# Preparing the second batch's second half later in the third chunk, with VectorE's and GpSimd's order held as written, in an attention kernel followed by an MLP

## The chip, the cores and the metric

The kernel runs on one core of one Trainium2 chip. The metric is the time of one execution on the device, in microseconds; lower is better. Times are given as the median of several executions. The profile and the trace come from one further execution of the same program.

## The reference

There are four batches, eight heads, 768 positions and 64 values per head. Queries and keys are hashed by the signs of six projections, and a query attends only to keys with the same six signs. The result goes through a layer norm, two matrix products with a rectifier between (512 to 2048 to 512), and a residual sum.

```python
q_bits = (np.einsum('bhsd,dk->bhsk', q, proj) > 0)        # the same for k
mask = q_bucket[:, :, :, None] == k_bucket[:, :, None, :]
scores = np.where(mask, scale * q @ k.T, -1e9)
attn = softmax(scores); x = attn @ v                       # heads side by side: 512 wide
xn = (x - mean) / sqrt(var + 1e-6) * g_ln
out = x + np.maximum(xn @ w_ch1, 0) @ w_ch2
```

## The kernel before

The work is cut into 12 chunks, numbered from 0: three for each batch, each with 256 query rows of all eight heads. A chunk's attention is 12 units, three for each pair of heads. A unit is `scores` (TensorE, L435), `exps` (ScalarE, L445), `values` (TensorE, L469, called av) and, after each third unit, `divide` (VectorE, L487 to L497). Scores and exponentials of the next unit are written ahead of the values of this one.

Between the units of chunk n the kernel places other work, called fillers:

- `norm` of chunk n-1: VectorE takes statistics (L516, L517) and writes xn (L518), for each of two rows; a transposing DMA on SyncE's queue, SP, makes xnT (L538); GpSimd makes rs, the inverse deviation (L529, L530). For chunk 1 the transposes are done by TensorE (`xtrans`, L550) and copied by VectorE (L557).
- eight `down` steps of chunk n-2 (L590, four products each). The last of each four is followed by L595, in which VectorE takes the sum o out of PSUM, and by a store.
- eight `up` steps of chunk n-1 (L566, eight products each), whose results VectorE (L576) and ScalarE (L578) rectify in turn.
- preparation of a later batch, by half (four heads). A step's letter is followed by batch and half, so that N11 is the narrowing of batch 1, half 1, which is the second batch's second half.

The preparation's letters: L and W load queries, keys, and values (SP's queue); Q takes squares on ScalarE; N narrows queries and keys to bf16 on GpSimd (two casts, L282); B transposes 32-wide blocks on VectorE (four, L287); T issues a transposing DMA on SP and a copy from it (L304, L309); H is 32 hash products on TensorE (L318), two VectorE instructions for the bits (L326, L329), and one store and four loads on SP (L331, L333); V casts values (L344) and sums them (L351, L353) on GpSimd; E is one product on TensorE (L358, share) and a VectorE copy (L359). Products of hashes, shares, xnT's transposes, ups and downs all take one of two PSUM buffers with the tag mm.

`plan` says what chunk n prepares. What stands before the bar is spread over the first four downs, what stands behind it over the last four, and `interleave` then places the whole list by the costs given with each step (a down counts 870, an up 900, hash products 1300, a share 110, the rest nothing). The rest of the written order is in `interleave`: a unit's scores and exponentials, fillers, values, divide, fillers.

The written order is binding only where `tc.manual_schedule` holds an engine. In chunks 0 and 1 (`first_two`) all engines are held. From chunk 2 on only ScalarE is held, and the framework's scheduler chooses at build time the order in which the other engines and SP's queue get their instructions. `tc.no_sync_barrier()` stands between the chunks. The norm, downs and ups after the last chunk stand outside any held block.

Chunk 9 ends with `safety`: VectorE reduces the squares (L647), TensorE transposes the result (L650), and VectorE makes a flag of it (L652 to L656). It costs 0 in the list and stands last in it.

```python
fillers = [norm]
fillers += mixed(early, tail[:4]) + ([(600, xtrans)] if n == 2 else [])
fillers += mixed(late, tail[4:]) + ups
...
with tc.manual_schedule(engines={mybir.EngineType.Activation}):
    interleave(units[n], fillers, after, single)
```

Of the kernel before, what the change touches and what calls it, by code (L numbers as in the profile page):

```python
# [30 lines left out]
def kernel(  # L31
# [629 lines left out]
    def interleave(units, fillers, after=None, single=()):  # L661

        total = sum(c for c, _ in fillers) or 1
        slots_n = 2 * len(units)
        done, fi = 0.0, 0

        def fill(upto):
            nonlocal done, fi  # L670
            while fi < len(fillers) and done <= upto * total:
                c, f = fillers[fi]
                f()
                done += c
                fi += 1

        for u, (_, _, values, divide) in enumerate(units):
            nxt = units[u + 1] if u + 1 < len(units) else after
            if nxt:
                nxt[0]()  # L680
                nxt[1]()
            fill((2 * u + 1) / slots_n)
            if u % 2 and u // 2 < len(single):
                for _, f in single[u // 2]:
                    f()
            values()
            divide()
            fill((2 * u + 2) / slots_n)
        while fi < len(fillers):
            fillers[fi][1]()  # L690
            fi += 1
# [4 lines left out]
    def chunk_tile():  # L696
        return work.tile([P, TT, d_model], F32, tag="x", bufs=3, name="x")
# [18 lines left out]
    def first_two():  # L716
# [76 lines left out]


    plan = {
        2: "H10 N11 B11 V10 W11 | T11 H11 E10 V11 W20",
        3: "E11 N20 B20 | T20 H20",
        4: "V20 W21 B21 N21 | T21 H21 E20",
        5: "V21 W30 | E21",
        6: "V30 W31 N30 B30 | T30 H30 E30",  # L800
# [7 lines left out]
    def prepare(text):  # L808
        return [
            step  # L810
            for op in text.split()
            for step in preps[int(op[1])].part(op[0], half=int(op[2]))
        ]

    def mixed(a, b):

        tagged = [((i + 1) / (len(a) + 1), 0, i, s) for i, s in enumerate(a)]
        tagged += [((i + 1) / (len(b) + 1), 1, i, s) for i, s in enumerate(b)]
        return [s for *_, s in sorted(tagged, key=lambda e: e[:3])]
# [6 lines left out]
    for n in range(2, len(chunks)):  # L826
        tc.no_sync_barrier()
        mlp[n - 1] = mlp_steps(*chunks[n - 1], xs[n - 1])
        norm, ups, downs, xtrans, _ = mlp[n - 1]
        early, late = (prepare(part) for part in (plan.get(n, "") + "|").split("|")[:2])  # L830
# [3 lines that stand above are left out]
        tail = downs  # L834
        if n == NT * (B - 1):
            fillers.append((0, safety))
        after = None
        if n + 1 < len(chunks):
            xs[n + 1] = chunk_tile()
            units[n + 1] = att_units(*chunks[n + 1], xs[n + 1])  # L840
            after = units[n + 1][0]
        single = [[step] for step in prepare(singly.get(n, ""))]
        if len(single) > 4:
            single[3:] = [sum(single[3:], [])]
        with tc.manual_schedule(engines={mybir.EngineType.Activation}):
            interleave(units[n], fillers, after, single)
    tc.no_sync_barrier()
    norm, ups, downs, _, _ = mlp_steps(*chunks[-1], xs[len(chunks) - 1])
# [188 lines left out]
```

## Time and profile before

| what | value |
|---|---|
| three runs | 321.61, 322.49, 322.43 us, median 322.43 |
| the profiled execution | 322.48 us |
| its span in the profile | 320.6 us |
| TensorE busy | 303.1 us, 95% of the span |
| ScalarE, VectorE, GpSimd busy | 216.6, 186.8, 85.0 us |
| DMA | 40.93 MB, 128 GB/s on average |

The span runs from the first to the last instruction of the profile; what lies around it makes up the rest of the execution's time. In the profile PE is TensorE's products and PEld its weight loads, DVE is VectorE, ACT ScalarE, POOL GpSimd, and SPq SyncE's queue, which issues most of the DMAs. L435 is line 435 of the kernel. An arrow in brackets behind a timeline row gives the idle time of that engine just before it, and what ended it. The granted clock is TensorE's, as a share of full speed. A busy TensorE is not TensorE at its peak, since its products are pipelined and their ends are modelled.

### The profile page before, as it was taken

The page shows a single profiled execution, that of the slowest core. Times are in us where ns is not written, and L with a number is a line of the kernel's source. Part 1 is how long each engine was busy: PE and PEld are TensorE (multiplying, and loading weights), DVE is VectorE, ACT ScalarE, POOL GpSimd, SP SyncE. Part 2 cuts the span into 40 slices and gives each one's busy share as a digit, 9 for nine tenths or more (in the row PEclk, how much of TensorE's full clock was granted, in tenths as well). Part 3 has the DMA queues.
Part 4 walks back from the last instruction along what each step waited for, and adds up shares of the span by engine and source line. Part 5 has one row for each costly group of instructions (what it writes and reads, how often), then busy time and mean ns, then how long its engine had stood idle before and what let it go on. Part 6 is the DMA issues. An engine that isn't in the chain of part 4 may idle for free.

```text
span 320.6 us, 7775 instructions
## 1 busy us (share of the span) xinstructions
PE 303.1 (95%) x3225; PEld 226.5 (71%) x3252; DVE 186.8 (58%) x403; ACT 216.6 (68%) x272; POOL 85.0 (27%) x110
## 2 busy tenths in 40 slices
PE   7979999799999998999999999999999999999991
PEld 6566687469669656868768768769679688686650
DVE  1799987833893772456596675543634734446320
ACT  4677976558668764778778678779788568564110
POOL 3467522850330280057082040100200200201000
PEclk9999999989999997999999999999999999999997
DMA  7999999978577597824984452020120210200301
GB/s 249 353 199 301 209 341 109 152 193 177 166 145 212 154 171 195 251 75 147 255 129 81 84 111 60 2 69 34 30 72 2 65 35 2 65 35 2 99 13 63
DMA packets 64826, 40.93 MB, mean 128 GB/s; under 512 B 47136, under 2 KB 59680, under 8 KB 64784
## 3 DMA queue, kind: packets, MB, share of 16 engines
q1 hardware_dynamic: 60368, 31.85, 41.5%
q0 software_dynamic: 4128, 8.13, 10.9%
q8 instruction: 27, 0.44, 0.6%
q10 hardware_dynamic: 288, 0.39, 0.3%
q14 instruction: 15, 0.12, 0.1%
HBM read 27.98 MB, written 6.88 MB: 109 GB/s over the span
## 4 chain that ended last, share of the span: by engine, by line
PE 81%; DVE 12%; DMA 2%; ACT 1%; issue 1%; POOL 0%; SPq 0%; POOLq 0%
PE hp L566 27%; PE o L590 20%; PE sc L435 17%; PE av L469 10%; DVE xn L518 3%; PE hash L318 3%; DMA xnT<-xn 2%; DVE bt L287 2%; PE tpose L200 2%; DVE slots L262 2%; PE wakep L731 1%; DVE slots L238 1%; DVE stats L516 1%; PE hash L252 1%; DVE x L497 1%
## 5 line engine op out<-in xcount | busy, mean ns | idle before, releaser
L445 ACT ACTIVATE ex<-sc,expb 128x1024 bf16<-128x1024 f32 x144 | 159.4, 1113 | 65.1 <-PE sc L435 62.6
L566 PE MATMUL hp<-xnT,w_sb 128*128 128x256 bf16 x768 | 99.8, 274 | 2.6 <-DMA xnT<-xn 2.3
L590 PE MATMUL o<-w_sb,hbuf 128*128 128x512 bf16 x357 | 92.6, 379 | 3.3 <-DVE x L595 2.2
L435 PE MATMUL sc<-slots 70*128 70x256 bf16 x576 | 87.0, 273 | 2.4 <-POOL slots L238 1.5
L566 PEld LDWEIGHTS <-w_sb 128*128 128x128 bf16 x768 | 72.2, 98 | 12.1 <-DMA xnT<-xn 3.0
L469 PEld LDWEIGHTS <-ex 128*128 128x128 bf16 x1152 | 54.5, 98 | 16.0 <-issue 1.5
L576 DVE TENSOR_SCALAR hbuf<-hp 128x512 bf16<-128x512 f32 x48 | 33.1, 690 | 54.6 <-PE hp L566 54.4
L435 PEld LDWEIGHTS <-slots 70*128 70x128 bf16 x576 | 52.1, 97 | 17.1 <-issue 3.7
L469 PE MATMUL av<-vaug,ex 128*128 128x65 bf16 x1152 | 59.2, 194 | 0.3 <-ACT ex L445 0.2
L590 PEld LDWEIGHTS <-hbuf 128*128 128x128 bf16 x384 | 35.5, 97 | 30.1 <-issue 2.6
L529 POOL TENSOR_SCALAR rs<-mv 128x2 f32<-128x2 f32 x12 | 6.3, 523 | 144.2 <-DVE mv L517 144.0
L578 ACT ACTIVATE hbuf<-hp 128x512 bf16<-128x512 f32 x48 | 28.5, 594 | 18.7 <-PE hp L566 18.5
L595 DVE SCALAR_TENSOR_TENSOR x<-o,rs,x 128x512 f32<-128x512 f32 x24 | 17.8, 741 | 34.5 <-PE o L590 34.5
L518 DVE SCALAR_TENSOR_TENSOR xn<-x,mv,gbc 128x512 bf16<-128x512 f32 x24 | 21.7, 927 | 0.1
L497 DVE TENSOR_TENSOR x<-x,rc 128x256 f32<-128x256 f32 x36 | 19.0, 529 | 0.9
L282 POOL CAST nat<-qnat 128x1536 bf16<-128x1536 f32 x6 | 9.0, 1501 | 36.4 <-DMA qnat<-in_q_dram 24.6
L516 DVE BATCH_NORM_STATS2 stats<-x 128x6 f32<-128x512 f32 x24 | 15.4, 681 | 0.3
L490 DVE TENSOR_TENSOR x<-av,vsum 128x256 f32<-128x256 f32 x36 | 14.9, 414 | 0.0
L489 DVE TENSOR_SCALAR rc<-av 128x4 f32<-128x4 f32 x36 | 5.7, 158 | 15.7 <-PE av L469 15.7
L344 POOL CAST vaug<-vnat 128x1536 bf16<-128x1536 f32 x8 | 11.8, 1474 | 8.0 <-PE av L469 4.0
L180 ACT ACTIVATE knat<-knat 128x768 f32<-128x768 f32 x16 | 13.4, 835 | 0.0
L180 ACT ACTIVATE qnat<-qnat 128x768 f32<-128x768 f32 x16 | 13.3, 833 | 0.0
(83 smaller groups left out, 215.1 us busy)
## 6 DMA issues: line engine op xcount, KB each, us to landing
out_dram<-x SPq DMA_DIRECT2D x24, 256.0 KB
vnat<-in_v_dram SPq DMA_DIRECT2D x7, 768.0 KB
qnat<-in_q_dram SPq DMA_DIRECT2D x11, 384.0 KB
knat<-in_k_dram SPq DMA_DIRECT2D x11, 384.0 KB
w_sb<-in_moe_w_ch_dram POOLq DMA_DIRECT2D x4, 1024.0 KB, 14.0
slots<-slots SPq DMA_DIRECT2D x6, 384.0 KB
qnat<-in_q_dram POOLq DMA_DIRECT2D x2, 768.0 KB, 14.5
knat<-in_k_dram POOLq DMA_DIRECT2D x2, 768.0 KB, 15.9
```

The lines of the kernel that those rows point to most:

```text
L180: nc.scalar.activation(src, src, AF.Square, accum_out=sq[:, a, col : col + 1],)
L435: nc.tensor.matmul(sc[:, i, :], key_block(h, kj), query_blocks(h),)
L445: nc.scalar.activation(ex, sc, AF.Exp, bias=expb[:, 1:2] if b else expb[:, 0:1], scale=scale if b else scale / Q_SCALE,)
L469: nc.tensor.matmul(av[:, h - ha, qi, :], state[g][:, i, qi * P : (qi + 1) * P], va[:, h, kj, :], start=(b > 0 and (g, i, qi) == (0, 0, 0)) ...
L497: nc.vector.tensor_tensor(xv, num, rc.unsqueeze(3).to_broadcast([P, 2, TT, D]), op=AOP.mult)
L516: nc.vector.bn_stats(stats, x[:, i, :])
L518: nc.vector.scalar_tensor_tensor(xn[:, :, i, :], x[:, i, :].rearrange("p (o d) -> p o d", d=P), mv[:, i, 0:1], gbc.rearrange("p (o d) -> p ...
L566: nc.tensor.matmul(hp[:, i, :], w1_sb[:, dt, nt * P : (nt + 1) * P], st["xnT"][:, dt, :], start=(dt == 0), stop=(dt == ND - 1),)
L576: nc.vector.tensor_scalar_max(dst, src, 0.0)
L578: nc.scalar.activation(dst, src, AF.Relu)
L590: nc.tensor.matmul(o2, st["h"][:, nt, i * P : (i + 1) * P], w2_sb[:, nt, :], start=(nt == 0), stop=(nt == NH - 1),)
L595: nc.vector.scalar_tensor_tensor(x[:, i, :], o2, st["rs"][:, i : i + 1], x[:, i, :], op0=AOP.mult, op1=AOP.add,)
```

## The change

Two edits. In chunk 2 the steps V10, W11, B11 and N11 move behind the bar, in this order, so that they are spread over the last four downs, ahead of T11, H11, E10 and V11; of the early ones only H10 stays before the bar. W20 moves from the end of chunk 2 to the start of chunk 3. And from chunk 2 on the written order is binding for VectorE and GpSimd as well as for ScalarE; TensorE and SP are left to the scheduler as before.

```diff
     plan = {
-        2: "H10 N11 B11 V10 W11 | T11 H11 E10 V11 W20",
-        3: "E11 N20 B20 | T20 H20",
+        2: "H10 | V10 W11 B11 N11 T11 H11 E10 V11",
+        3: "W20 E11 N20 B20 | T20 H20",
         4: "V20 W21 B21 N21 | T21 H21 E20",
...
-        with tc.manual_schedule(engines={mybir.EngineType.Activation}):
+        with tc.manual_schedule(
+            engines={
+                mybir.EngineType.Activation, mybir.EngineType.DVE, mybir.EngineType.Pool
+            }
+        ):
             interleave(units[n], fillers, after, single)
```

## The prediction

> **What bounds the kernel now.** I read the page's busy table first, then the windows cut at the chunk boundaries, then the list of waits, then the timeline of the two stretches that stand out. Chunks are counted from 0 as in the code; chunk 2 is the third.
>
> ```profile
> PE 303.1 (95%) x3225; PEld 226.5 (71%) x3252; DVE 186.8 (58%) x403; ACT 216.6 (68%) x272; POOL 85.0 (27%) x110
> ```
>
> TensorE is the bound, with 17.5 us idle in 320.6. An order can only win where TensorE stands still or is throttled, so I cut the span where each chunk's first BATCH_NORM_STATS2 starts (columns: us, then busy us of PE, PEld, DVE, ACT, POOL, granted clock, DMA share, GB/s).
>
> ```profile
> 51.80:82.60 30.80, 28.44 (x321) 20.88 (x323) 17.38 (x31) 19.12 (x26) 13.95 (x16) 0.94 0.78 160
> 82.60:107.40 24.80, 24.30 (x272) 18.29 (x275) 17.43 (x36) 18.69 (x26) 8.07 (x7) 1.00 0.60 149
> 107.40:135.20 27.80, 25.63 (x272) 18.87 (x274) 15.93 (x36) 18.61 (x25) 7.15 (x9) 0.94 0.84 208
> 205.10:227.30 22.20, 22.09 (x240) 17.00 (x240) 10.70 (x29) 18.21 (x25) 1.71 (x2) 1.00 0.13 38
> ```
>
> The last row is chunk 8, with nothing to prepare: 22.2 us is the floor. Chunk 4 has one set of hash products (1.5 us) and a share (0.3) more, so about 24.0; it took 27.8. Chunk 2 has two sets, two shares, 0.6 of transposes and 0.6 of extra av products, so about 27.0; it took 30.8. Chunk 3 is 0.8 over. From chunk 5 on nothing is lost. So some 8 us can be won, nearly all in chunks 2 and 4. The timeline names the causes:
>
> ```profile
> 58.15 1.03 PE L590 MATMUL o<-w_sb,hbuf 128*128 128x512 bf16 x4
> 59.56 1.82 DVE L287 STREAM_TRANSPOSE bt<-knat 128x768 f32<-128x768 f32 x2
> 61.83 0.74 DVE L595 SCALAR_TENSOR_TENSOR x<-o,rs,x 128x512 f32<-128x512 f32 x1
> 62.62 1.02 PE L590 MATMUL o<-w_sb,hbuf 128*128 128x512 bf16 x3 [2.20 <-DVE x L595]
> ```
>
> Chunk 2: the first o was complete at 59.2, but L595, which empties its PSUM buffer, stood behind block transposes (L287) that the scheduler had put ahead of it; TensorE waited 2.20 us.
>
> ```profile
> 111.34 0.71 DVE L518 SCALAR_TENSOR_TENSOR xn<-x,mv,gbc 128x512 bf16<-128x512 f32 x1
> 113.44 3.69 SPq L304 DMA_TRANSPOSE slots<-nat  x1
> 117.23 1.26 SPq L538 DMA_TRANSPOSE xnT<-xn  x1
> 121.62 1.64 PE L566 MATMUL hp<-xnT,w_sb 128*128 128x256 bf16 x8 [2.01 <-DMA xnT<-xn]
> ```
>
> Chunk 4: xn was ready at 112.05, but its transposing DMA stood on SP behind that of L304, which itself waited for GpSimd's cast until 113.40. TensorE waited 2.01 us. Each hole also costs clock:
>
> ```profile
> 60.48:63.90 3.42, 1.22 (x7) 1.00 1.10 213
> 118.51:121.92 3.41, 1.40 (x11) 1.00 1.14 157
> 19.52:22.94 3.42, 1.91 (x18) 1.00 1.09 183
> ```
>
> (us, PE busy, clock.) After the first two stretches the clock is half for 3.41 us, 63.9 to 67.3 and 121.9 to 125.3: half of 3.41, 1.7 us, each. After the third, busy 1.91 of 3.42, it stays full.
>
> The Trainium skill ("TensorE: Matmul & The Clock Gate", Part 1) has the clock halve after an idle window of about 3.4 us. By that rule gaps of 2 us would cost no clock and 3.4 us less could be won (about 321.8 in place of the forecast below); the granted 0.94 in both chunks contradicts it, so the rows decide and it gets no chance.
>
> **The change, part by part.** The sum is made against the profiled execution's own 322.48 us (span 320.6, 1.9 outside), 0.05 above the median.
>
> *Chunk 2, plan and VectorE's order.* Written out, VectorE's order is: both norm rows, bits of H10, divide of unit 2, L595 of the first o, copy of xnT, then the four blocks. L595 then starts when the o ends and TensorE has scores, eight transposes and one unit's av (1.25 us) to run meanwhile. The casts N11, beside which the two xn took 3.76 us (1.40 where GpSimd was quiet), move behind values and sums. Gain: 2.2 + 1.7 = 3.9. What is late next: H11 needs the four blocks, which now start near 60.6 and end near 64.4 (4 x 0.95), against a written place near 63.8 on TensorE. Bounds: 0, if the hash is queued behind other ready products, to 2.2, the old hole; I take 0.5, nearest to the 0.2 to 0.3 that hashes waited before.
>
> *Moved steps at nothing.* H10 passes two groups of down products; its bits still reach SP by about 57.5 instead of 61.7 and are needed only at the end of chunk 2. T11 (SP 3.7 to 4.2 us, then the copy L309) moves from 57.4 to about 64 on SP; bits of H11, its store and four loads stay near 68 to 77; the half is needed by unit 6 of chunk 3, near 89: 10 us of cover, beyond which each us would stop TensorE. W11 leaves SP some 4 us earlier, since values10 is done sooner. W20, a SP load, moves from 72.5 to chunk 3's start; its values are cast only in chunk 4. V11's sums finish near 69, share 11 comes near 81.
>
> *Chunk 3.* The four loads L20 stand on SP behind the bits of H11 in both versions (77.07 to 79.15), so they land at about the same absolute time, K by 86.4 at the latest; but chunk 3 starts some 3 us sooner. Held VectorE then waits at the blocks, with L595 and a divide behind it: last block near 89.7, against about 88.8 where TensorE reaches H20. Loss 0 to 2; I take 0.9, less 0.3 of the present excess: +0.6.
>
> *Chunk 4.* GpSimd's written order is rs of the norm, values20, its sums, then the two casts of N21. So the cast can no longer be scheduled ahead of the norm, and the scheduler, which still orders SP, sees xnT ready 8 us before L304. The norm without blocks between takes about 3.2 us (2 x (0.65 + 0.16 + 0.75)), xnT leaves near 3.3 us into the chunk instead of 9.6, and lands 4.35 later, before the ups at 12. Gain 2.0 + 1.7 = 3.7.
>
> *Chunks 4, 6, 7, the held queues.* GpSimd used to run values and sums ahead, in chunks 3 and 5; now all of it (9 us: 1.3 + 1.5 + 3.4 + 3.0) follows the norm. The four blocks come before or around L595, so the hash can be late by what VectorE loses. Bounds 0 to 2.2 each; I take 0.3 each, 0.9 in all.
>
> *Chunk 9, safety.* It is written last, behind unit 11's divide, and VectorE is now held.
>
> ```profile
> 242.16 0.19 DVE L647 TENSOR_REDUCE m<-sq 128x2 f32<-128x32 f32 x1 [0.46 <-ACT knat L180]
> 248.17 0.38 PE L650 MATMUL mp<-identf,m 128*1 128x128 f32 x2
> 248.37 0.16 DVE L489 TENSOR_SCALAR rc<-av 128x4 f32<-128x4 f32 x1 [1.12 <-PE av L469]
> ```
>
> The reduction L647 was done 6 us early. Now it starts after the divide that begins at 248.37 and takes 1.0, ends near 249.6, and mp can start at 249.65 instead of 248.17. Engines do not cross chunk barriers (VectorE idled 2.1 us before 154.6, with a block of chunk 6 ready), so TensorE waits: +1.5. Its stretch stays about 58% busy, where the clock held. If scores of chunk 10 could pass, it would be 0; if the clock drops, 3.2.
>
> *Chunks 8, 10, 11* show VectorE already in written order, apart from interleaved norm rows: 0. The last norm stands outside the held block.
>
> Sum: -3.9 + 0.5 + 0.6 - 3.7 + 0.9 + 1.5 = -4.1, so 318.4.
>
> **Rivals.** (a) Only chunk 4's hole closes; chunk 2's moves to H11 at its full size: -3.7 + 0.6 + 0.9 + 1.5 = -0.7, 321.8. For it: the blocks are four in a row just before the hash; against it: downs and scores are ready to fill. (b) The held queues cost nothing and safety hides: -7.6, 314.9; against it: 242.16 and 248.17 above. (c) Slower: GpSimd's bunched run beside VectorE. x L497 took 1.58 us at 164.83 beside a cast, 0.42 alone, and xn 1.88 against 0.70. If in chunks 3, 4, 6 and 7 this makes L595 and blocks late at a TensorE order that doesn't allow for it, each loses 2.2 and, where a stretch falls under half busy, 1.7: four times 2.2 and once 1.7 is 10.5 in place of the 1.5 counted, +4.9, 327.4. It decides from 5.6 lost there, 1.4 a chunk. The Trainium skill ("SBUF — State Buffer", on the shared port pair) says a VectorE instruction with two SBUF inputs and a GpSimd one that reads SBUF exclude each other for a whole instruction; the trace agrees (1.58 against 0.42). Against (c): block transposes keep 0.94 to 0.97 either way. (d) The order changes nothing: excluded, since the trace's order differs from the written one at both holes.
>
> **Numbers.** Forecast 0.56, own range 316.5 to 320.5; (a) 0.16, two thirds of it faster by over 0.3%; (b) 0.05; (c) 0.21, part of it only just slower; the rest, 0.02, is cancellation. Faster 0.70, same 0.08, slower 0.22. 0.3% (1 us) is about what a measurement of this kernel tells from no change. The range runs from 315.5 to 323.6, leaving out most of (b) and (c).
>
> **What would show it.** Right: no wait of PE o L590 on DVE x L595 and none of PE hp on xnT before the last chunk, granted clock 1.00 in chunks 2 and 4, about 27.7 and 24.3 us for them, L538 before L304 in chunk 4, m after the last divide of chunk 9 with 1.5 us of idle TensorE before mp. Wrong: a clock of 0.5 anywhere between 50 and 290 us, hash products that wait over 1 us, or TensorE waiting for slots.

## The result, and the profile after

The changed kernel takes 323.38 us (median of 20 executions, 321.41 to 325.53), the kernel before 322.14 (20 executions, 320.57 to 323.87). The ratio is 1.0045 with a 95% interval of 1.0023 to 1.0066: it is slower by about half a per cent, where the prediction had it 1.3% faster. (The comparisons leave disturbed executions out, so a ratio need not be the quotient of two medians.) The profiled execution of after took 325.0 us, 323.0 of them span; it is one of the longer ones.

The page's busy table first:

```profile
PE 303.6 (94%) x3252; PEld 225.3 (70%) x3252; DVE 188.2 (58%) x403; ACT 216.6 (67%) x272; POOL 84.3 (26%) x110
```

TensorE is busy as long as before and idle 19.4 us in place of 17.5: the sum says nothing of what happened. The windows do. These are chunks 2 to 7 and 9 of after, cut where VectorE's last divide of the chunk before ends; chunk 9 is cut at the end of L654, a step of `safety`, where that comes later (columns: us, busy us of PE, PEld, DVE, ACT, POOL, granted clock, DMA share, GB/s):

```profile
52.14:79.33 27.19, 27.19 (x325) 20.20 (x324) 16.35 (x31) 19.47 (x27) 13.65 (x16) 1.00 0.60 142
79.33:105.78 26.45, 24.78 (x276) 18.40 (x275) 15.83 (x35) 18.61 (x25) 4.38 (x4) 1.00 0.80 187
105.78:130.42 24.64, 24.04 (x275) 18.04 (x273) 17.63 (x35) 18.32 (x25) 9.07 (x10) 1.00 0.81 185
130.42:156.59 26.17, 24.08 (x243) 17.74 (x241) 11.50 (x30) 18.16 (x25) 6.22 (x8) 0.93 0.52 154
156.59:181.41 24.82, 24.48 (x275) 18.12 (x273) 16.96 (x36) 18.34 (x25) 9.24 (x10) 1.00 0.50 117
181.41:206.05 24.64, 24.02 (x275) 18.02 (x273) 17.66 (x35) 18.31 (x25) 9.08 (x10) 1.00 0.41 88
228.23:251.63 23.40, 22.09 (x242) 17.07 (x240) 11.73 (x31) 17.75 (x25) 1.49 (x2) 1.00 0.13 35
```

In the first row TensorE is busy all of the time at full clock. The dip to 0.94 in chunks 2 and 4 is gone, and a dip to 0.93 stands in chunk 5. Cut in the same way, the chunks of all the kernels take (us, from one profiled execution each; chunk 8 takes 22.15 to 22.18 and chunk 11 takes 21.71 to 21.73 in every one). The prediction's cuts lie up to 0.25 us earlier, so its rows for chunks 2 to 4 of before differ a little from the first row here.

| kernel | c2 | c3 | c4 | c5 | c6 | c7 | c9 | c10 |
|---|---|---|---|---|---|---|---|---|
| before | 31.03 | 24.73 | 27.64 | 22.26 | 23.82 | 23.82 | 22.41 | 22.26 |
| after | 27.19 | 26.45 | 24.64 | 26.17 | 24.82 | 24.64 | 23.40 | 22.60 |
| e1_plan_only | 28.54 | 25.08 | 27.58 | 22.28 | 23.81 | 23.81 | 22.40 | 22.27 |
| e2_hold_only | 27.36 | 27.85 | 24.65 | 26.37 | 24.80 | 24.65 | 23.41 | 22.60 |
| e3_pool_free | 27.20 | 24.34 | 24.41 | 22.27 | 26.40 | 24.15 | 23.42 | 22.60 |
| e4_share_later | 27.19 | 25.99 | 24.64 | 22.16 | 25.17 | 24.63 | 23.41 | 22.60 |
| e5_safety | 27.19 | 25.30 | 24.64 | 24.52 | 24.82 | 24.64 | 22.57 | 22.15 |
| e6_chunk3_late | 27.19 | 24.21 | 26.01 | 26.17 | 24.79 | 24.63 | 23.41 | 22.60 |
| e7_three | 27.19 | 24.66 | 27.97 | 22.16 | 25.18 | 24.65 | 22.56 | 22.15 |
| e8_all_late | 27.19 | 24.21 | 25.45 | 22.16 | 25.40 | 25.39 | 22.57 | 22.16 |
| e9_dve_to_four | 27.19 | 24.53 | 24.15 | 22.28 | 23.80 | 23.82 | 22.40 | 22.27 |
| e10_both_to_four | 27.19 | 26.11 | 24.66 | 22.28 | 23.81 | 23.81 | 22.40 | 22.27 |
| e11_pool_not_five | 27.19 | 26.04 | 24.64 | 22.28 | 24.81 | 24.64 | 23.42 | 22.59 |
| e12_dve_old_plan | 28.55 | 24.62 | 24.16 | 22.27 | 23.82 | 23.80 | 22.40 | 22.26 |

The second row less the first: chunk 2 -3.84, chunk 4 -3.00, together -6.84 won; chunk 3 +1.72, chunk 5 +3.91, chunks 6 and 7 +1.82, chunks 9 and 10 +1.33, together 8.78 lost; with 0.34 before chunk 2 that is +2.3 of the 2.4 us between the spans.

The two holes of before are closed. Chunk 2, the timeline:

```profile
59.62 0.75 DVE L595 SCALAR_TENSOR_TENSOR x<-o,rs,x 128x512 f32<-128x512 f32 x1 [0.29 <-PE o L590]
60.60 1.03 PE L590 MATMUL o<-w_sb,hbuf 128*128 128x512 bf16 x4
61.05 1.83 DVE L287 STREAM_TRANSPOSE bt<-qnat 128x768 f32<-128x768 f32 x2
64.41 1.51 PE L318 MATMUL hash<-bt,proj 128*32 128x192 f32 x32
```

L595 now waits for the o, not the o for L595; the blocks come behind it, and the hash products behind those without a wait. Chunk 4, VectorE and SP's queue:

```profile
108.37 0.75 DVE L518 SCALAR_TENSOR_TENSOR xn<-x,mv,gbc 128x512 bf16<-128x512 f32 x1
109.19 1.30 SPq L538 DMA_TRANSPOSE xnT<-xn  x1
118.00 3.65 SPq L304 DMA_TRANSPOSE slots<-nat  x1
```

The transpose of xn leaves SP 0.07 us after xn is ready and 8.8 us ahead of L304, behind which it stood before.

What took their place is in the list of TensorE's waits (us in total, times, longest):

```profile
PE share L358 <- POOL vs L353: 2.1, 1, 2.1
...
PE hash L318 <- DVE x L595: 1.4, 3, 1.0
PE mp L650 <- DVE m L647: 1.3, 1, 1.3
PE hp L566 <- DVE vsum L359: 1.1, 3, 0.4
...
PE hash L318 <- DVE bt L287: 0.7, 1, 0.7
```

The largest, 2.1 us at a share, is in chunk 5, where the prediction had looked for nothing.

### The profile page after: what moved, and what is told of

Its sections match the earlier page's. It is cut to its first block, busy times and chain, and to the rows that moved or that the text cites. A ratio compares the mean times of both kernels' runs of the same rounds, so it can differ in the third digit from the quotient of the medians.

```text
span 323.0 us, 7803 instructions
## 1 busy us (share of the span) xinstructions
PE 303.6 (94%) x3252; PEld 225.3 (70%) x3252; DVE 188.2 (58%) x403; ACT 216.6 (67%) x272; POOL 84.3 (26%) x110
## 4 chain that ended last, share of the span: by engine, by line
PE 65%; DVE 15%; DMA 9%; POOL 5%; ACT 2%; issue 2%; SPq 0%; POOLq 0%; DVEq 0%; ACTq 0%
PE hp L566 24%; PE o L590 15%; PE sc L435 13%; PE av L469 8%; DVE bt L287 2%; DVE xn L518 2%; DVE stats L516 2%; PE hash L318 2%; DMA proj<-in_proj_dram 2%; DMA qnat<-in_q_dram 2%; DVE x L497 2%; DMA slots<-nat 2%; DVE slots L262 2%; DMA slots<-slots 1%; POOL vsum L353 1%
## 5 line engine op out<-in xcount | busy, mean ns | idle before, releaser
L566 PE MATMUL hp<-xnT,w_sb 128*128 128x256 bf16 x768 | 98.7, 272 | 1.6 <-DVE vsum L359 1.1
L590 PE MATMUL o<-w_sb,hbuf 128*128 128x512 bf16 x384 | 97.4, 382 | 0.0
L529 POOL TENSOR_SCALAR rs<-mv 128x2 f32<-128x2 f32 x12 | 9.1, 759 | 193.1 <-DVE mv L517 193.1
L595 DVE SCALAR_TENSOR_TENSOR x<-o,rs,x 128x512 f32<-128x512 f32 x24 | 17.8, 741 | 32.9 <-PE o L590 31.0
L518 DVE SCALAR_TENSOR_TENSOR xn<-x,mv,gbc 128x512 bf16<-128x512 f32 x24 | 17.9, 751 | 0.8
L497 DVE TENSOR_TENSOR x<-x,rc 128x256 f32<-128x256 f32 x36 | 17.5, 487 | 1.2
L516 DVE BATCH_NORM_STATS2 stats<-x 128x6 f32<-128x512 f32 x24 | 16.5, 690 | 0.4
L287 DVE STREAM_TRANSPOSE bt<-qnat 128x768 f32<-128x768 f32 x12 | 11.2, 956 | 2.8 <-DMA qnat<-in_q_dram 2.8
L353 POOL TENSOR_TENSOR vsum<-vsum,vaug 128x256 f32<-128x256 f32 x18 | 12.0, 667 | 1.4
```

The source lines that it names most:

```text
L497: nc.vector.tensor_tensor(xv, num, rc.unsqueeze(3).to_broadcast([P, 2, TT, D]), op=AOP.mult)
L516: nc.vector.bn_stats(stats, x[:, i, :])
L518: nc.vector.scalar_tensor_tensor(xn[:, :, i, :], x[:, i, :].rearrange("p (o d) -> p o d", d=P), mv[:, i, 0:1], gbc.rearrange("p (o d) -> p ...
L566: nc.tensor.matmul(hp[:, i, :], w1_sb[:, dt, nt * P : (nt + 1) * P], st["xnT"][:, dt, :], start=(dt == 0), stop=(dt == ND - 1),)
L590: nc.tensor.matmul(o2, st["h"][:, nt, i * P : (i + 1) * P], w2_sb[:, nt, :], start=(nt == 0), stop=(nt == NH - 1),)
L595: nc.vector.scalar_tensor_tensor(x[:, i, :], o2, st["rs"][:, i : i + 1], x[:, i, :], op0=AOP.mult, op1=AOP.add,)
```

## The experiments

Each kernel is given as its edit against the changed kernel, except where the text names another (the engines' names shortened), what was expected, and what came out; the times of its chunks are in the table above.

**e1_plan_only** leaves the new plan and takes the new holds away.

```diff
-        with tc.manual_schedule(engines={Activation, DVE, Pool}):
+        with tc.manual_schedule(engines={Activation}):
```

> The new plan with only ScalarE held, as before. Theory A (the held orders carry both the gains and the losses; the plan does little): SP still gets L304 ahead of L538 in chunk 4, so that hole of 2.0 us and its half clock stay; L595 in chunk 2 still stands behind four blocks; no wait of the share in chunk 5, none of mp in chunk 9. About 322 us, within 1.5 of before. Rival B (the move of the preparation makes the loads of L20 late and that is the loss): chunk 3 over 26 us instead of 24.7, and slower than before by 1 to 2 us.

320.6 us against 321.72 of before, ratio 0.998 (0.9942 to 1.0018): no difference that these runs resolve. Chunk 4 keeps its hole (27.58; TensorE waits 2.0 us for xnT). Chunk 2 takes 28.54 in place of 31.03 even so: the wait at L595 is 1.2 us in place of 2.2, and the clock does not drop.

**e2_hold_only** leaves the holds and takes the new plan away.

```diff
-        2: "H10 | V10 W11 B11 N11 T11 H11 E10 V11",
-        3: "W20 E11 N20 B20 | T20 H20",
+        2: "H10 N11 B11 V10 W11 | T11 H11 E10 V11 W20",
+        3: "E11 N20 B20 | T20 H20",
```

> The old plan, with VectorE and GpSimd held. Theory A: chunk 4's hole closes (-3.0), chunk 5 gets the wait of the share for GpSimd's sums (+4.0), chunks 6 and 7 lose 1.7, safety 1.4; chunk 2 keeps part of its hole, since the blocks are written ahead of L595. About 324 to 326 us. Rival B: without the move of the plan the loss of chunk 3 is gone and it is faster than the changed kernel, about 321.

327.4 us, ratio 1.0188 (1.014 to 1.0236): slower, and by more than after. The holds alone are enough for the gain and for the loss. Chunk 2 takes 27.36 and chunk 4 takes 24.65 without the plan; chunks 5 to 10 lose what after loses. Chunk 3 is worse than in after, 27.85 (a share waits for GpSimd's sums there too, 0.69 us), so it isn't the plan that made the loads of L20 late.

**e3_pool_free** holds VectorE and ScalarE, and lets GpSimd go.

```diff
-            engines={Activation, DVE, Pool}
+            engines={Activation, DVE}
```

> The changed kernel with GpSimd free and only ScalarE and VectorE held. Theory A: GpSimd runs its values and sums ahead again, so TensorE's share product in chunk 5 doesn't wait: the 2.1 us and the half clock (1.7) there go, about 319.5 us; chunk 9 keeps its 1.4. Rival C (VectorE's held order alone is the loss, by late hash products and block transposes): chunk 5 stays near 26 us and the time stays at 323.4.

319.96 us, ratio 0.9936 (0.9905 to 0.9966): faster than before. Chunk 5 is back at 22.27 and chunk 3 at 24.34, so both losses came with GpSimd's hold. But chunk 6 now takes 26.40: the hash products wait 1.15 us, and the ups 0.77 more. The timeline there:

```profile
157.31 1.47 POOL L344 CAST vaug<-vnat 128x1536 bf16<-128x1536 f32 x1
157.55 1.50 DVE L497 TENSOR_TENSOR x<-x,rc 128x256 f32<-128x256 f32 x1
158.98 0.97 DVE L287 STREAM_TRANSPOSE bt<-knat 128x768 f32<-128x768 f32 x1
160.00 0.84 PE L318 MATMUL hash<-bt,proj 128*32 128x192 f32 x12 [1.15 <-DVE bt L287]
```

A divide beside GpSimd's cast took 1.50 us (0.42 in after, at 163.70), the last block came that much later, and TensorE stood in the middle of the hash products (last row). That is the mechanism of rival (c), at one place and 1.15 us large there. The Trainium skill ("SBUF — State Buffer", on the shared port pair) has a VectorE instruction with two SBUF inputs and a GpSimd one that reads SBUF exclude each other; the trace agrees, 1.50 against 0.42.

**e4_share_later** moves the share of chunk 5 into chunk 6, all three engines held.

```diff
-        5: "V21 W30 | E21",
-        6: "V30 W31 N30 B30 | T30 H30 E30",
+        5: "V21 W30 |",
+        6: "E21 V30 W31 N30 B30 | T30 H30 E30",
```

> The changed kernel with the share of batch 2's second half (E21) moved from chunk 5 to the start of chunk 6, which changes no engine's hold. Theory A: the wait of L358 on L353 and the half clock after it go; chunk 5 takes 22.2 us instead of 26.2, chunk 6 at most 0.5 more; about 319.5 us. Rival D (the wait of the share stands in place of another that would be there anyway, such as xnT's DMA, issued at 134.65 behind the loads): chunk 5 keeps 1 us or more of idle TensorE and the time falls by less than 2.5.

320.25 us, ratio 0.9955 (0.9924 to 0.9987). Chunk 5 takes 22.16: with the share out of the way the hole and the drop are gone, though GpSimd's sums are as late as in after. Chunk 6 takes 0.35 more.

**e5_safety** writes `safety` two places earlier.

```diff
-            fillers.append((0, safety))
+            fillers.insert(len(fillers) - 2, (0, safety))
```

> The changed kernel with safety written two ups earlier in chunk 9, so that its reduction stands ahead of the last divides on VectorE. If the 1.31 us that TensorE waited for L647 are the whole price of safety, chunks 9 and 10 go from 23.40 and 22.60 to about 22.4 and 22.3, 1.3 us less in all, and nothing else moves: about 322 us. Rival: the wait only moves, because VectorE now waits for TensorE's mp product ahead of an up's rectifying, and chunk 9 stays over 23 us.

322.0 us, ratio 0.9994 (0.9962 to 1.0025). Chunks 9 and 10 take 1.28 less than in after, about what the step was counted at (1.5). Chunk 5 had the same wait of 2.09 us at the share and yet took 24.52, not 26.17, since the clock did not drop; the last section says why.

**e6_chunk3_late** writes narrowing and blocks of chunk 3 behind the bar, when their loads have landed.

```diff
-        3: "W20 E11 N20 B20 | T20 H20",
+        3: "W20 E11 | N20 B20 T20 H20",
```

> The changed kernel with chunk 3's N20 and B20 moved behind the bar, so that the blocks stand after the first four downs and after the first L595. If chunk 3's loss is VectorE, held, waiting for the late loads of L20 with L595 and the hash behind it, chunk 3 goes from 26.45 us to about 24.3 and the time falls by 2, to about 321.4. Rival: the hash products come too late for something else (SP's copy and the loads of L21 behind them), and chunk 4 loses what chunk 3 gains.

324.97 us, ratio 1.0111 (1.0057 to 1.0165). Chunk 3 takes 24.21 with TensorE never idle, but chunk 4 takes 26.01, where the hash products wait:

```profile
PE hash L318 <- DVE x L595: 2.0, 1, 2.0
```

Chunk 3 won 2.24 and chunk 4 lost 1.37 against after: a part of the loss moved into chunk 4, as the rival had it, though by another wait than the one it named. By its median this kernel is slower than after, which its one profile, an execution below the median, does not explain.

**e7_three** takes the edits of e4, e5 and e6 together.

> The changed kernel with three places mended: the share E21 in chunk 6, safety two ups earlier, chunk 3's N20 and B20 behind the bar. If the three losses are separate, chunks 3, 5 and 9 with 10 take 24.3, 22.2 and 44.7 us, and the time is 323.4 less 3.1, 1.9 and 1.3, about 317. If they share a cause, the sum of the savings is less than 5 us.

321.65 us, ratio 0.9986 (0.9952 to 1.0019), where 317 was expected. Chunks 3, 5 and 9 with 10 take 24.66, 22.16 and 44.71, about as expected. But chunk 4 takes 27.97, with a wait of 2.4 us of the hash products for L595 and a drop of the clock: what e6 handed on to chunk 4 eats up the rest.

**e8_all_late** is e7 with the blocks and the narrowing behind the bar in chunks 4, 6 and 7 as well (chunks 4 and 7 are shown).

```diff
-        4: "V20 W21 B21 N21 | T21 H21 E20",
+        4: "V20 W21 | B21 N21 T21 H21 E20",
...
-        7: "V31 B31 N31 | T31 H31 E31",
+        7: "V31 | B31 N31 T31 H31 E31",
```

> As the kernel with three places mended, and in chunks 4, 6 and 7 too the blocks and casts (B and N) behind the bar. If what those chunks still lose (0.6, 1.1 and 0.6 over 24.0) is L595 behind four block transposes on held VectorE, they take about 24.1 each and the time is about 315.5. Rival: it is GpSimd's casts beside VectorE, which are there in any order, and the chunks stay where they are: 317.

319.59 us, ratio 0.9952 (0.9916 to 0.9988). Chunks 4, 6 and 7 take 25.4 each, more than in after and far from what was expected: the blocks now stand ahead of the second L595, and the ups (hp) wait for it, three times, 2.2 us in all. Moving the blocks only traded one consumer against another here.

**e9_dve_to_four** holds VectorE in chunks 2 to 4 alone, GpSimd never.

```diff
-            engines={Activation, DVE, Pool}
+            engines={Activation, DVE} if n <= 4 else {Activation}
```

> The plan of after, with VectorE held beside ScalarE in chunks 2 to 4 only; GpSimd never, and from chunk 5 on ScalarE alone, as before. Theory: what the change wins is won in chunks 2 to 4 by VectorE's order alone, and everything from chunk 5 on that it loses (share in 5, hash and hp waits in 6 and 7, safety in 9 and 10: +7.1 in the trace of after against before) comes from orders held where nothing was to be won. So chunks 2, 3 and 4 take 27.2, 24.3 and 24.4 us as in the kernel with GpSimd free (7.5 under before's 83.4), and chunks 5 to 11 what they took before (22.3, 23.8, 23.8, 22.15, 22.4, 22.3, 21.7): about 315 us against 322.1. Rival: chunk 4's end hands less on to chunk 5 than before's (values and narrowing not run ahead), so that 5 to 7 lose 2 to 4 us whatever order is held there: 317 to 319.

315.62 us, ratio 0.9834 (0.9787 to 0.9881): the fastest of all, 5.8 us under the 321.46 of before beside it. The clock doesn't drop inside the chunks, and no chunk from 5 on differs from before by more than 0.03. Its windows for chunks 2 to 4:

```profile
52.36:79.55 27.19, 27.19 (x325) 20.19 (x324) 16.81 (x31) 19.47 (x27) 12.04 (x15) 1.00 0.65 142
79.55:104.08 24.53, 24.53 (x276) 18.40 (x275) 16.75 (x36) 18.62 (x25) 7.02 (x6) 1.00 0.82 210
104.08:128.23 24.15, 23.96 (x275) 18.03 (x273) 16.68 (x35) 18.32 (x25) 8.18 (x10) 1.00 0.68 167
```

TensorE is idle for 0.19 us in these 76. The rival (chunks 5 to 7 lose 2 to 4 us whatever is held there) falls.

**e10_both_to_four** holds GpSimd too, in chunks 2 to 4.

```diff
-            engines={Activation, DVE, Pool}
+            engines={Activation, DVE, Pool} if n <= 4 else {Activation}
```

> The plan of after, with VectorE and GpSimd both held beside ScalarE in chunks 2 to 4, ScalarE alone from chunk 5 on. Theory: chunks 2 to 4 as in after (27.2, 26.4, 24.6; 5.1 under before), chunk 5 without the wait at the share, since GpSimd's order is free again there, and the rest as before: about 317. If holding GpSimd is what makes chunk 3 take 26.4 in place of 24.3, the kernel with VectorE alone held in 2 to 4 is 2 us faster than this one. Rival: the values of chunk 5 are late because GpSimd could not run ahead in chunk 4, not because it is held in chunk 5; then the share waits here too, 2 us of idle TensorE and with a clock drop 3.7: 319 to 321.

317.13 us, ratio 0.9884 (0.984 to 0.9928), where about 317 was expected. Beside e9 on the same chip it is 1.5 us longer, and chunk 3 (26.11 against 24.53) and chunk 4 (24.66 against 24.15) more than account for it. Chunk 5 takes 22.28 without a wait at the share: its cast, no longer held, runs at 117.30, in chunk 4, straight behind the last cast held there. So what made the share late was that the instructions of chunk 5 were held, not those of chunk 4.

**e11_pool_not_five** lets GpSimd go in chunk 5 alone.

```diff
-            engines={Activation, DVE, Pool}
+            engines={Activation, DVE} if n == 5 else {Activation, DVE, Pool}
```

> After, with GpSimd set free in chunk 5 alone. Theory: GpSimd's casts and sums of that chunk come ahead of, or between, the norm's two instructions, the share stops waiting, and chunk 5 takes 22.2 in place of 26.2; all other chunks as in after (27.2, 26.4, 24.6, then 24.8, 24.6, 22.2, 23.4, 22.6): about 319.4, 3.9 under after and just faster than before by more than 0.3%. Rival: chunk 6 takes over what 5 no longer waits for (it took 26.4 with GpSimd free everywhere): 321.

320.55 us, ratio 0.999 (0.9957 to 1.0024). Chunk 5 takes 22.28 in place of 26.17 and nothing is handed on to chunk 6 (24.81); the other chunks are after's. The profiles of the two differ by 3.9 in chunk 5 alone, but the medians by 2.8, and the two ratios to before (1.0045 and 0.999) by only 1.8 us; a part of after's executions may not have the whole loss (last section).

**e12_dve_old_plan** is e9 with the plan of before (the edit is against e9).

```diff
-        2: "H10 | V10 W11 B11 N11 T11 H11 E10 V11",
-        3: "W20 E11 N20 B20 | T20 H20",
+        2: "H10 N11 B11 V10 W11 | T11 H11 E10 V11 W20",
+        3: "E11 N20 B20 | T20 H20",
```

> The plan of before, with VectorE held beside ScalarE in chunks 2 to 4 only; GpSimd never, and ScalarE alone from chunk 5 on. It differs from the kernel with VectorE held in 2 to 4 and the plan of after (315.6 us) by the plan alone. Theory: VectorE's order is what closes both holes, so chunks 2 and 4 take about 27.3 and 24.3 us with this plan too, and the plan matters only through SP: with both queues held, the old plan had the loads of L20 leave SP some 3 us later than the new one (qnat at 83.25 against 80.48) and chunk 3 took 27.85 against 26.45. So chunk 3 takes between 24.5 (GpSimd's free order makes the loads early enough) and 26 us: 316 to 317.5, under before by over 1%. Rival: the plan is half of the gain; with the old one chunk 2 keeps a hole at L595 or at the hash products, because values and casts of the second half stand ahead of the blocks, and the kernel takes 318 to 320.

316.47 us, ratio 0.9849 (0.9799 to 0.9898), inside the range expected. The interval overlaps e9's, so the runs don't tell the two plans apart; the profiles differ in chunk 2 alone (28.55 against 27.19), where an o still waits 1.3 us for L595. Nearly all of the gain is VectorE's order in three chunks.

## Why the prediction was wrong

**Chunk 2 and chunk 4: the holes closed; half of the account was needed.** Chunk 2 gave 3.84 where 3.9 less 0.5 was counted (the hash products did not wait at all); chunk 4 gave 3.00 where 3.7 less 0.3 was (two waits, 0.19 and 0.41, are left). That is 6.84 against 6.8, and it is luck that the two differences cancel.

In chunk 2 the causes overlap: the plan alone gave 2.49 (e1), the holds alone 3.67 (e2), VectorE's hold with the old plan 2.48 (e12) and with the new one all of it (e3, e9). Of each of these 1.7 is the clock, which drops in chunk 2 of before alone. In chunk 4 the plan alone gave nothing (e1), so a hold did it. But the prediction closed this hole by GpSimd's written order, which keeps the cast, and so L304, behind the norm. e9 closes it with GpSimd free, and takes 24.15 in place of 24.64:

```profile
106.67 0.75 DVE L518 SCALAR_TENSOR_TENSOR xn<-x,mv,gbc 128x512 bf16<-128x512 f32 x1
107.48 1.30 SPq L538 DMA_TRANSPOSE xnT<-xn  x1
110.33 3.67 SPq L304 DMA_TRANSPOSE slots<-nat  x1
```

The other half of the account, no blocks between the norm's rows, is what remains: xn is ready 3.3 us into the chunk here, as in after, and 4.5 us into it before. VectorE's hold was enough; GpSimd's was not needed. Why the scheduler then puts L538 ahead on SP is not shown further.

One caution on the size: the prediction's sum was made against a profiled execution in which the clock dropped in both chunks. Its mean granted clock was 0.983. Of the 86 executions of before that ran beside the experiments, 20 were below 0.986 (median 323.5 us), 41 at 0.986 to 0.990 (321.6) and 25 above (320.7). The execution that was read was thus among the most throttled, and the 3.4 us of clock in the sum is likely more than a typical one has to give.

**Chunk 5: the step that failed.** The prediction's step "Chunks 4, 6, 7, the held queues" says that GpSimd ran values and sums ahead in chunks 3 and 5, which is work for chunks 4 and 6, and prices the loss of that at 0.3 in each of 4, 6 and 7. It passes over the same run-ahead in chunk 4, where the cast of V21 ran for chunk 5, and so chunk 5 is in the sum at nothing. Chunk 5 lost 3.91, nearly the whole net gain of 4.1 that was forecast. After, GpSimd and TensorE:

```profile
133.07 0.78 POOL L529 TENSOR_SCALAR rs<-mv 128x2 f32<-128x2 f32 x1 [15.09 <-DVE mv L517]
134.59 1.48 POOL L344 CAST vaug<-vnat 128x1536 bf16<-128x1536 f32 x1
139.11 0.65 POOL L353 TENSOR_TENSOR vs<-vsum,vaug 128x256 bf16<-128x256 f32 x1
139.81 0.27 PE L358 MATMUL share<-vs,epsk 128*128 128x256 bf16 x1 [2.09 <-POOL vs L353]
```

and before, with the cast still in chunk 4:

```profile
117.29 1.50 POOL L344 CAST vaug<-vnat 128x1536 bf16<-128x1536 f32 x1
136.82 0.64 POOL L529 TENSOR_SCALAR rs<-mv 128x2 f32<-128x2 f32 x1 [17.33 <-DVE mv L517]
140.67 0.66 POOL L353 TENSOR_TENSOR vs<-vsum,vaug 128x256 bf16<-128x256 f32 x1
142.33 0.27 PE L358 MATMUL share<-vs,epsk 128*128 128x256 bf16 x1
```

Counted from the chunk's start (135.20 before, 130.42 after): before, the sums were done at 6.1 and the share came at 7.1, 1.0 to spare, because the cast had run in chunk 4 (117.29) and only the sums were left. After, GpSimd stood idle for 15.09 us, since rs of the norm is written ahead of that cast (in e10 and e11, where chunk 5 is free, the cast ran at 117.30 and 117.12 without a wait, so its data were there); the whole chain of rs, cast and sums then ended at 9.3, and TensorE reached the share at 7.3. TensorE lost 2.09, and 1.7 more by the clock. This could have been worked out from the trace of before: rs started 1.6 us into the chunk, and rs, cast and sums one behind the other (0.64 + 0.72 + 1.50 + 0.62 + 1.02 + 1.39 + 0.66 = 6.55) make 8.2, against a share at 7.1. The rest of the wait is, by the traces, VectorE's hold: rs needs the statistics of both rows, and with the first row's xn written between them it started 2.65 us into the chunk. By the prediction's own times for the norm's steps that start is at 2.4, which makes the end 8.9, a wait of 1.8. Three experiments show it by different means: GpSimd free everywhere (e3), GpSimd free in chunk 5 (e11) and the share elsewhere (e4) each bring chunk 5 to 22.2 or 22.3.

**Chunk 3: mis-sized, +0.6 forecast, +1.72 measured.** The step held that the four loads L20 leave SP at the same time as before. Three of them left later, at 79.93 to 81.32 in place of 77.57 to 78.68. The traces put this down to a chain that starts on GpSimd. After, the second cast of N11, L304 and the third load on SP:

```profile
62.79 1.47 POOL L282 CAST nat<-knat 128x1536 bf16<-128x1536 f32 x1
64.29 3.55 SPq L304 DMA_TRANSPOSE slots<-nat  x1
80.48 0.80 SPq L138 DMA_DIRECT2D qnat<-in_q_dram  x1
```

and in e9, where GpSimd is free to narrow before the sums:

```profile
57.98 1.47 POOL L282 CAST nat<-knat 128x1536 bf16<-128x1536 f32 x1
59.48 4.35 SPq L304 DMA_TRANSPOSE slots<-nat  x1
77.87 0.47 SPq L138 DMA_DIRECT2D qnat<-in_q_dram  x1
```

L304 starts 0.03 us behind the cast in both, and 2.6 of the 4.8 us between the two casts still separate the loads. That GpSimd's hold makes the loads late is shown by e9 and e10; the steps of the chain are read from the traces, and SP's own order, which the scheduler sets anew in each kernel, differs as well. In after VectorE then stands at a block for its data, with L595 and a divide queued behind, and TensorE waits twice:

```profile
86.73 0.98 DVE L287 STREAM_TRANSPOSE bt<-qnat 128x768 f32<-128x768 f32 x1 [2.84 <-DMA qnat<-in_q_dram]
88.49 0.71 DVE L595 SCALAR_TENSOR_TENSOR x<-o,rs,x 128x512 f32<-128x512 f32 x1
89.26 1.17 PE L318 MATMUL hash<-bt,proj 128*32 128x192 f32 x20 [1.00 <-DVE x L595]
91.09 0.84 PE L318 MATMUL hash<-bt,proj 128*32 128x192 f32 x12 [0.66 <-DVE bt L287]
```

The wait itself, 2.84 us at a block, was described in the prediction with its place; the price, 0.9, was low for this execution, as the hash products waited for L595 and again for the last block. e9 and e10 differ in GpSimd's hold alone and in chunk 3 by 1.58.

The size itself varies. After, e4, e5, e10 and e11 have the same order up to here, and chunk 3 took 26.45, 25.99, 25.30, 26.11 and 26.04, which is 0.57 to 1.72 over before. In e5 the load of the second qnat left SP 1.24 us into the chunk, about as in after (1.15), but its block could start 1.4 us sooner; TensorE then waited once, 0.57. So the forecast of 0.6 lies at the low end of what the profiles show, and after's 1.72 at the high end.

**Chunks 6 and 7: +1.82 measured, 0.6 forecast.** The hash products and the ups wait in turn, 0.2 to 0.45 us at a place, three places in chunk 6 (weight loads included) and two in chunk 7. Setting both engines free there (e9, e10) takes both chunks back to 23.8; setting GpSimd free alone (e3) doesn't (26.40 and 24.15). VectorE's hold is thus part of the cause; no run sets VectorE alone free there.

**Chunk 9, safety: right.** 1.33 in chunks 9 and 10 where 1.5 was counted, by the wait described:

```profile
249.34 0.16 DVE L489 TENSOR_SCALAR rc<-av 128x4 f32<-128x4 f32 x1 [1.12 <-PE av L469]
250.30 0.18 DVE L647 TENSOR_REDUCE m<-sq 128x2 f32<-128x32 f32 x1
250.62 0.38 PE L650 MATMUL mp<-identf,m 128*1 128x128 f32 x2 [1.31 <-DVE m L647]
```

**The rivals.** (a) and (b) did not happen: chunk 2's hole closed fully, and the held queues did cost. (c) put the slower side on bunched GpSimd work slowing VectorE down. That such a slowing made TensorE wait was found once, in e3; after's largest loss has another cause, a wait on GpSimd's own results. The test written beforehand ("a clock of 0.5 anywhere between 50 and 290 us, hash products that wait over 1 us") did show it: the clock was 0.5 from 140.50, and the longest wait of the hash products was 1.00 us, at 89.26.

## What to carry to other kernels

Holding an engine to a written order removes the scheduler's mistakes and its run-ahead together, so it should be held only in the stretches whose profile shows a hole that the order causes: here VectorE in three of ten chunks was worth 1.5 to 1.7%, and both engines in all ten were a loss. Before an engine is held, take for every consumer on the bounding engine the chain that now stands behind the engine's first wait, add up its durations from the chunk's start, and compare with the moment when the consumer is reached; here the loss fell on the one that used to have 1 us to spare. Price an engine's order also by the queues that it feeds: with a cast 4.8 us later on GpSimd, the loads of the next chunk left SP 2.6 us later.

## What the runs showed of the hardware

The same hole can cost 2.1 us or 3.8. The profiled executions of after and e5 both idle for 2.09 us at the share of chunk 5. In all 14 profiles the granted clock changes only at steps of 3.413 us, counted from its first rise (3.96 us into the span in after, 3.80 in e5). In after the hole lies within one step, which is the first row here; the second is the next step:

```profile
137.08:140.50 3.42, 1.33 (x9) 0.78 (x8) 0.38 (x1) 2.13 (x4) 2.45 (x4) 1.00 1.02 260
140.50:143.91 3.41, 3.41 (x19) 1.76 (x17) 0.05 (x1) 1.27 (x2) 0.00 (x0) 0.50 0.92 347
```

In e5 it lies across a border:

```profile
133.51:136.92 3.41, 2.38 (x22) 1.52 (x21) 0.98 (x5) 2.67 (x5) 3.09 (x5) 1.00 0.88 226
136.92:140.34 3.42, 2.35 (x21) 1.46 (x21) 0.42 (x1) 0.90 (x2) 0.94 (x2) 1.00 0.99 344
```

A step with TensorE busy for 1.33 of 3.42 us (39%) is followed by one at half clock; two steps at 69 and 70% are not. The 14 profiles agree on every step behind the first rise: each one with TensorE busy for 43% or less is followed by half clock (13 steps at 16 to 43%, besides the idle end of the span), and each one at 51% or more by full clock; between the two nothing was measured. The Trainium skill ("TensorE: Matmul & The Clock Gate", Part 1) calls the window free-running, which agrees; it speaks of an idle window, where here a window that is 39% busy is enough. So whether a hole of 2 us costs clock depends on where it falls against these steps, and the first rise, from which they count, lay anywhere from 3.80 to 7.05 us into the span. Of after's 20 executions 7 have a mean granted clock of 0.996 or more and a median of 322.35 us, the other 13 have 0.993 or less and 323.8; the profiled one, at 0.992, is of the second kind. That the drop in chunk 5 is what separates the two was not shown, as only one of the 20 has a trace.
